# A fused attention, router and feed-forward kernel: set-up moved to GpSimd, identity transposes added, and the order of the expert stage's side work changed

## The chip, the cores and the metric

The kernel runs on one core of one Trainium2 chip. The metric is the device time of one execution in microseconds; before the change three executions took 980.26, 981.56 and 983.67 us (median 981.56). One more execution was profiled: it took 980.59 us, of which 978.8 us lie between its first and its last instruction (the span). Engine names: PE is TensorE's matrix products and PEld its weight loads, DVE is VectorE, ACT is ScalarE, POOL is GpSimd, SP is the engine that issues most transfers.

## What is computed

Three parts run one after the other, all in float32:

```python
# attention: 4 batches, 8 heads, 576 positions, 64 columns a head
scores = q @ k.T / sqrt(64)
keep   = scores >= scores.max(-1) - tau          # others count as minus infinity
x      = softmax(scores where kept) @ v          # reshaped to 2304 tokens x 512
# one of 8 experts for each token
logits = x @ w_gate + modality_bias[modality_id]
e      = argmax(logits);  g = softmax(logits)[e]
x      = g * (relu(x @ w1[e]) @ w2[e])           # 512 -> 1024 -> 512
# a dense layer for all tokens
h = x @ w_in                                     # 512 -> 2048
out = (h * sigmoid(1.702 * h)) @ w_out           # 2048 -> 512
```

Most products are made of several products of rounded parts (a high and a low part of each operand), so that the float32 accuracy is kept.

## The kernel before

**Attention** goes over 16 pairs of heads, four a batch, with nine units of work a pair. `Attention.run` (from L404) handles two units in each pass of its loop, so there are 72 passes and one closing pass; pass numbers below count from 0. In a pass, TensorE makes the scores of two units (`qk`, L234) into one of two PSUM buffers, and transposes the masked scores of the two units of the pass before (`trans`, L302). VectorE takes the row maximum (`max`, L245), ScalarE the exponential (`exp`, L251), VectorE the mask and row sum (`mask`, L275), which frees the PSUM buffer for the next scores but one. After that come a few matrix products with V from a list (`avq`), work on the rows of a finished half batch (`rowq`), and one entry of `poolq`, then the list `side`.

`poolq` holds the preparation of the operands of later pairs (`split`, L137): for each half of a pair's columns GpSimd scales the query rows (L143), rounds keys and queries into `kA` (L144) and forms the rest `kB` (L145). After the second half, `place` issues four transfers on SP (L154 to L157) that bring the parts to the partitions where they are multiplied; L156 writes over what L154 reads, and L157 over what L155 reads. In pass 0 four entries are put there, two for pair 1 and two for pair 2; one entry runs in each pass. Pair 1 is first used by the second unit of pass 4.

Each engine takes its instructions in the order in which the program issues them, and there is no planner: the order is written out by hand, with constants for how many entries of each list a pass takes.

`side` is a list of small pieces of work that `sides(n)` (L492) takes from the front, up to n at a call; a `None` ends the call, and is taken off. During attention a pass takes one. At the start the list holds seven `None`, then `gate_setup`, the clearing of a block of rows that is then written to memory ten times (`extra`), and the router's seven set-up pieces (`setup_items`, L543: `loads`, `ids`, `parts`, `tables`, `order`, `modality`, `bias`), which prepare counters, comparison tables and the bias of each token. These fall into passes 19 to 25. Later entries are the router's own work on a batch (`gate_items`) and, after the third and the fourth batch, the assignment of tokens to slots of 512 rows of one expert (`assign`, phases A and B).

**Assignment B** ranks the tokens of each expert, finds a place for each, and turns places into lists of token numbers. It compares a counter with each token's place to build `OL` (`low`, L845, three instructions), builds `R` (`high`, L851), multiplies `R` by two tables of token number digits (`values(0)` and `values(1)`, L858, both on GpSimd in phase B), and multiplies `OL` with `R` on TensorE (`sum_up`), from which `lists` makes the indices called `gB`.

**The expert stage** has five slots s of eight steps f each (the loop from L1308). In a step (`Ffn.step`) TensorE multiplies the tokens with 128 columns of w1 (`s1`, 12 products, L945), ScalarE and VectorE form the rounded activation and its rest (L1149, L1150), and TensorE makes the second product of the step two before (`s2`, 12 products, L967), in which the second product of the first group already needs the low part of w2 (`bl`). The weights of the next steps are split into high and low parts by ScalarE and VectorE (`split` in `slot`, L1185, L1186). In steps 3 to 6 the next slot's tokens are transposed (`xprep`, L929, into the one PSUM buffer `av`), copied by ScalarE (L931) and completed by VectorE (L932); the next transpose waits for the buffer. Meanwhile the dense layer's weights, 64-bit numbers, are read and converted (`convert`, L1078 to L1105) in 15 pieces that go through `Pipe` `conv`: load, `upper` (three VectorE operations, L1090 to L1092), `lower` (four, L1101 to L1105). `conv` starts a piece in each odd step and does its halves as it goes. Each step also calls `sides` twice, with 9 after the first product's activation and with 12 at its end, and so works off assignment B from slot 0 on. Slot 2 is the first that needs `gB`: at slot 1, step 1, the program takes from `side` until `gB` is there.

**The dense layer** goes over the tokens in five blocks of 16 steps, with the same `Ffn`, and converts what is left of the weights in its first block.

Of the kernel before, what the change touches and what calls it, by code (L numbers as in the profile page):

```python
# [8 lines left out]
F32 = mybir.dt.float32  # L9
# [4 lines left out]
ACTF = mybir.ActivationFunctionType  # L14
ALU = mybir.AluOpType
# [6 lines left out]
NE = 8  # L22
# [3 lines left out]
PJ = 9  # L26
# [6 lines left out]
NS0 = 7  # L33
# [3 lines left out]
HO = True  # L37
# [2 lines left out]
NBW = 6  # L40
F0 = (0, 1, 0)
NROW = 2
SN = 1
SD = (1, 2, 2, 2, 1)
TAU_MAX = 104.0
# [2 lines left out]
class Attention:  # L48
# [88 lines left out]
    def split(self, p, i, pieces):  # L137

        nc = self.nc
        d = self.st[p]  # L140
        n = 640 // pieces
        A, B_, F = (self.heads(d[x], n, i * n) for x in ("kA", "kB", "F"))
        nc.gpsimd.tensor_scalar_mul(F[64:128], F[64:128], self.cq[64:128, 0:1])  # L143
        nc.gpsimd.tensor_copy(A, F)  # L144
        nc.gpsimd.tensor_sub(B_, F, A.bitcast(F32))  # L145
        if i == pieces - 1:
            self.place(p)
# [256 lines left out]
    def run(self):  # L404
        nc = self.nc
        NU = NPAIR * UPP
        self.load_first()
        self.load(1)
        rest = self.first()
        self.load_v(0)  # L410
        self.load_v(1)
        self.load(2)
        self.poolq = []
        self.avq, self.rowq, self.side = avq, rowq, side = [], [], []
        side += [None] * NS0 + [self.gate_setup, *self.extra] + self.router.setup_items(self.setup)
        it = done = 0
        while done < NU:
            last = it >= IT_LAST
            us = [u for u in (2 * it, 2 * it + 1) if u < NU]
            ts = [u for u in (2 * it - 2, 2 * it - 1) if 0 <= u < NU]  # L420
            starts = [u // UPP for u in us if u % UPP == 0]
            for p in starts:
                if p + 3 < NPAIR:
                    self.load(p + 3)
                if p + 2 < NPAIR:
                    self.load_v(p + 2)
                for n in range(1 if p == 0 else p + 2, min(p + 3, NPAIR)):
                    self.operands(n)
                    self.poolq += [lambda n=n, i=i: self.split(n, i, NPC) for i in range(NPC)]
            copies = []  # L430
            for i in range(2):
                if i < len(us):
                    self.qk(us[i])
                if i < len(ts):
                    copies += self.trans(ts[i])
                if i == 0 and not last:
                    n = AV1[it % 9]
                    while n and avq:
                        avq.pop(0)()
                        n -= 1  # L440
            for i in range(2):
                for c in range(2):
                    if CO[c] == 2 * i and c < len(copies):
                        copies[c]()
                if i < len(us):
                    self.max(us[i])
                    self.exp(us[i])
                for c in range(2):
                    if CO[c] == 2 * i + 1 and c < len(copies):
                        copies[c]()  # L450
                if last:
                    self.sides(SD[i], False)
            while rest:
                rest.pop(0)()
            for i, u in enumerate(us):
                self.mask(u)
                if last:
                    self.sides(SD[i + 2], False)
            n = AVL[it - IT_LAST] if last else AV[it % 9]
            while n and avq:  # L460
                avq.pop(0)()
                n -= 1
            for u in ts:
                self.trans_tails(u)
            n = ROWL[it - IT_LAST] if last else ROW[it % 9]
            while n and rowq:
                rowq.pop(0)()
                n -= 1
            n = 1
            while n and self.poolq:  # L470
                self.poolq.pop(0)()
                n -= 1
            self.sides(SD[4] if last else SN)
            for u in ts:
                done = u + 1
                p, w = divmod(u, UPP)
                if w == UPP - 1:
                    avq += self.av_items(p)
                    if p % 2:
                        avq.append(lambda b=p // HP, hh=p % HP // 2: rowq.extend(self.row_items(b, hh)))  # L480
            it += 1
# [33 lines left out]
PG = 512  # L515
# [7 lines left out]
class Router:  # L523
# [19 lines left out]
    def setup_items(self, tmp_pool):  # L543
# [56 lines left out]
            nc.vector.tensor_scalar(i2[:, 1], iaf, 63, None, op0=ALU.bitwise_and)  # L600

        def tables():
            nc.vector.tensor_copy(self.idp, i2)
            nc.vector.tensor_scalar(self.tri, self.iota, pf[:, 0:1], None, op0=ALU.is_gt)
            nc.vector.tensor_scalar(self.rev, self.iota[:, 0:NE], -1.0, float(NE), op0=ALU.mult, op1=ALU.add)

        def order():
            e = self.iota[:, 0:NE]
            nc.vector.tensor_tensor(
                self.before, e.unsqueeze(2).broadcast_to([128, NE, NE]), e.unsqueeze(1).broadcast_to([128, NE, NE]),  # L610
                op=ALU.is_gt)
            nc.vector.tensor_scalar_mul(self.pages, e, float(PG))

        def modality():
            nc.vector.tensor_copy(midf[0:64], mi[:, :, 0:PJ:2, 0])
            nc.vector.tensor_copy(midf[64:128, :, 0:4], mi[:, :, 1:PJ:2, 0])
            nc.vector.tensor_scalar(nmid, flat, -1.0, 1.0, op0=ALU.mult, op1=ALU.add)

        def bias():
            nc.vector.tensor_mul(self.bias, wide(flat.unsqueeze(2)), wide(bb[:, 1:2, :]))  # L620
            nc.vector.tensor_mul(tmp, wide(nmid.unsqueeze(2)), wide(bb[:, 0:1, :]))
            nc.vector.tensor_add(self.bias, self.bias, tmp)

        return [loads, ids, parts, tables, order, modality, bias]

    def gate_items(self, b, lgt):
        nc, wk = self.nc, self.c
# [64 lines left out]
    def assign(self, ph, gate):  # L692
# [161 lines left out]
            )  # L854

        def values(i):
            eng = nc.vector if i and first else nc.gpsimd
            eng.tensor_mul(R[:, :, i, :], R[:, :, 1, :], self.idp[:, i, 0:n].unsqueeze(2).broadcast_to([128, n, nh]))  # L858

        def sum_up(c0, c1):  # L860
# [129 lines left out]
def moe_kernel(ctx, tc, kq, v, tau, mid, w_gate, mod_bias, w1, w2, w_in, w_out, out):  # L990
    nc = tc.nc
# [316 lines left out]
    for s in range(NS):  # L1308
        blk = blocks[s]
        for f in range(8):  # L1310
            ffn.step(blk, f, (lambda: blk["split"](0, 1)) if f == 1 and HO else None, mid3=lambda: att.sides(9))
            f0 = F0[min(s, 2)]
            if s + 1 < NS and f in (f0, f0 + 1):
                if f == f0:
# [25 lines left out]
            if conv is None:  # L1340
                if not att.tail(6):
                    open_resident()
                    wi, wo = R["wi"], R["wo"]
                    conv = Pipe(
                        [piece("i", i, wi, i) for i in range(NWI)] + [piece("o", i, wo, i) for i in range(NWO)])
            elif f % 2 == 1 or len(conv.live) > 1:
                conv.step(f % 2)
            for _ in range((XP0 if s == 0 else XP)[f]):
                if xq:
                    xq.pop(0)()  # L1350
            att.sides(12)
    conv.drain()
    convert_loads(2)

# [127 lines left out]
```

## Time and profile before

| what | value |
|---|---|
| device time, three executions | 980.26, 981.56, 983.67 us |
| profiled execution | 980.59 us, span 978.8 us |
| PE busy | 930.2 us (95%) |
| PEld busy | 750.0 us (77%) |
| DVE busy | 556.3 us (57%) |
| ACT busy | 448.8 us (46%) |
| POOL busy | 237.7 us (24%) |
| mean granted clock of TensorE | 0.985 |

Busy time is the sum of an engine's instructions, as the profiler saw them; a busy PE is one with a product in its pipeline, not one at its peak. The granted clock is the share of full speed that the chip's throttle let TensorE have: 1.00 is 2.4 GHz, 0.50 is 1.2 GHz. In the rows below, a line such as L234 is a line of the kernel, `out<-in` names its tiles, x3 counts merged instructions, and a bracket gives the idle time of the engine just before and who ended it.

### The profile page before, as it was taken

How to read it: one execution, taken by the hardware profiler on the slowest of the kernel's cores; microseconds unless marked ns; L12 is line 12 of the kernel's file. 1: busy time of each engine (PE TensorE's matmuls, PEld its weight loads, DVE VectorE, ACT ScalarE, POOL GpSimd, SP SyncE). 2: the span in 40 equal slices, each digit the busy share in tenths (PEclk: the TensorE clock that was granted, in tenths of full speed). 3: DMA queues.
4: the chain of work that ended last, by engine and by line, in shares of the span. 5: the costliest groups of instructions: out<-in, count | busy, mean ns of one | idle time of the engine just before them, and what ended most of it. 6: DMA issues, size and time to landing. Idle time of an engine off the chain costs nothing. (4 is left out here: it accounts for less than half of the span.)

```text
span 978.8 us, 13986 instructions
## 1 busy us (share of the span) xinstructions
PE 930.2 (95%) x5009; PEld 750.0 (77%) x5009; DVE 556.3 (57%) x1194; ACT 448.8 (46%) x803; POOL 237.7 (24%) x322
## 2 busy tenths in 40 slices
PE   7899899999988969999999999999999999999994
PEld 6677777777765758878888888888888888888884
DVE  5888888888795497787766479961111111111110
ACT  4677677777775424444444434542222222222221
POOL 5935465576404422020302010010001000100100
PEclk7999999999999989999999999999999999999998
DMA  6766654655505434556555135330011000100100
GB/s 198 168 193 171 150 145 116 162 145 132 120 2 157 135 90 171 172 197 211 175 162 180 57 96 163 108 108 1 1 44 44 1 1 22 44 1 1 44 1 24
DMA packets 61307, 100.59 MB, mean 103 GB/s; under 512 B 9073, under 2 KB 32625, under 8 KB 61234
## 3 DMA queue, kind: packets, MB, share of 16 engines
q1 hardware_dynamic: 57394, 87.15, 31.1%
q0 software_dynamic: 3840, 12.50, 3.8%
q8 instruction: 42, 0.69, 0.3%
q14 instruction: 31, 0.25, 0.1%
HBM read 63.99 MB, written 17.23 MB: 83 GB/s over the span
## 5 line engine op out<-in xcount | busy, mean ns | idle before, releaser
L1161 DVE TENSOR_TENSOR hl<-sg,hh 128x512 fp32r<-128x512 f32 (+1 forms) x80 | 51.0, 638 | 242.9 <-ACT hh L1159 242.9
L1158 ACT ACTIVATE sg<-tr 128x512 f32<-128x512 f32 (+1 forms) x80 | 44.3, 554 | 208.4 <-PE tr L945 207.0
L245 DVE TENSOR_SCALAR_CACHE_REDUCE e<-sc,taue 128x576 f32<-128x576 f32 x144 | 116.3, 813 | 31.1 <-PE sc L234 27.3
L251 ACT ACTIVATE e<-e,thr 128x576 f32<-128x576 f32 x144 | 111.1, 776 | 31.3 <-DVE e L245 30.6
L234 PE MATMUL sc<-kA,qT 128*128 128x288 f32 x320 | 104.4, 342 | 20.7 <-DVE E L275 16.3
L945 PE MATMUL tr<-xh,wi_h 128*128 128x512 f32 (+1 forms) x320 | 120.6, 377 | 0.0
L945 PE MATMUL tr<-xh,wi_l 128*128 128x512 f32 (+1 forms) x320 | 118.8, 371 | 0.0
L945 PE MATMUL tr<-xl,wi_h 128*128 128x512 f32 (+1 forms) x320 | 118.7, 371 | 0.0
L967 PE MATMUL sc<-wo_h,hl 128*128 128x512 f32 x288 | 113.8, 395 | 0.0
L967 PE MATMUL sc<-wo_l,hh 128*128 128x512 f32 x288 | 113.7, 395 | 0.0
L967 PE MATMUL sc<-wo_h,hh 128*128 128x512 f32 x288 | 113.5, 394 | 0.0
L275 DVE SCALAR_TENSOR_TENSOR E<-sc,thr,e 128x576 f32<-128x576 f32 x128 | 103.4, 815 | 8.4 <-ACT e L251 5.0
L304 ACT COPY AT<-tr 128x512 f32<-128x512 f32 x128 | 73.9, 577 | 43.3 <-PE tr L302 43.2
L234 PE MATMUL sc<-kB,qT 128*128 128x288 f32 x320 | 91.2, 301 | 0.5 <-DVE kB L215 0.5
L234 PEld LDWEIGHTS sc<-kA,qT 128*128 128x128 f32 x320 | 61.7, 193 | 37.7 <-issue 21.9
L302 PE MATMUL tr<-ident,E 128*128 128x128 f32 x512 | 79.2, 278 | 0.0
L348 PE MATMUL av<-AT,V 128*64 128x288 f32 x512 | 76.7, 419 | 0.0
L945 PEld LDWEIGHTS tr<-xh,wi_l 128*128 128x128 f32 x320 | 60.2, 188 | 11.4
L945 PEld LDWEIGHTS tr<-xl,wi_h 128*128 128x128 f32 x320 | 60.3, 188 | 11.2
L945 PEld LDWEIGHTS tr<-xh,wi_h 128*128 128x128 f32 x320 | 60.2, 188 | 11.1
L302 PEld LDWEIGHTS tr<-ident,E 128*128 128x128 f32 x512 | 64.3, 144 | 0.6 <-DVE r L284 0.4
L967 PEld LDWEIGHTS sc<-wo_h,hl 128*128 128x128 f32 x288 | 54.0, 187 | 13.0
(215 smaller groups left out, 1754.2 us busy)
## 6 DMA issues: line engine op xcount, KB each, us to landing
ra<-in_moe_w_dram SPq DMA_DIRECT2D x20, 512.0 KB, 5.6
rb<-in_moe_w_dram SPq DMA_DIRECT2D x20, 512.0 KB, 3.8
F<-in_kq_dram SPq DMA_DIRECT2D x15, 640.0 KB, 5.3
cv_raw<-in_moe_w_in_dram SPq DMA_DIRECT2D x16, 512.0 KB, 5.0
cv_raw<-in_moe_w_out_dram SPq DMA_DIRECT2D x16, 512.0 KB, 3.6
V<-in_vp_dram SPq DMA_DIRECT2D x16, 320.0 KB, 4.9
kA<-kA SPq DMA_DIRECT2D x15, 320.0 KB, 3.4
kB<-kB SPq DMA_DIRECT2D x15, 320.0 KB, 3.5
```

What stands on the lines that cost most here:

```text
L234: nc.tensor.matmul(sc[:, hf, 0:288], l, d[kk][:, c0 + hf * 288:c0 + (hf + 1) * 288], start=(i == 0), stop=(i == len(ops) - 1),)
L245: nc.vector.tensor_scalar(e, d["sc", w][:, :, 0:288], self.taue[:, 0:1], 3.0e38, op0=ALU.add, op1=ALU.min, accum_out=thr)
L251: self.nc.scalar.activation(d["e", w], d["e", w], ACTF.Exp, bias=d["thr", w][:, 0:1], scale=-1.0)
L275: nc.vector.scalar_tensor_tensor(out=E.rearrange("p (a c) -> p a c", a=2), in0=d["sc", w][:, :, 0:288], scalar=d["thr", w][:, 0:1], in1=d[ ...
L302: nc.tensor.transpose(tp[:, kc * 128:(kc + 1) * 128], E[:, k0 + kc * 128:k0 + (kc + 1) * 128], self.ident)
L304: copies.append(lambda: nc.scalar.copy(AT[:, h, :, c * 128:(c + 1) * 128], tp.rearrange("p (k c) -> p k c", k=4)))
L348: nc.tensor.matmul(d["av"][h * 64:(h + 1) * 64, 0:288], d["V"][:, h, kc, :], d["AT"][:, h, kc, hf * 288:(hf + 1) * 288], start=False, stop ...
L945: nc.tensor.matmul(hps[:, 0:T], w[:, kd, :], blk[x][:, kd, :], start=(i == 0), stop=(i == 11))
L967: nc.tensor.matmul(y, h[:, cs], w, start=(f == 0 and i == 0), stop=(f == blk["nf"] - 1 and i == 2))
L1158: nc.scalar.activation(sg, hps, ACTF.Gelu_apprx_sigmoid)
L1161: return [upper, lambda: nc.vector.tensor_sub(hl, sg, hh.bitcast(F32))]
```

## The change

Seven edits are made together.

1. A list `FILL` gives numbers for passes 0 to 4 of attention; so many transposes of the identity matrix are issued in each of these passes after the masks, into the PSUM buffer `av`. Nobody reads their result.
2. For pair 1 alone, the scaling in `split` is issued on ScalarE in place of GpSimd. In pass 0 two entries of `poolq` run in place of one.
3. The router's set-up pieces come before the cleared rows in `side`, so they fall into passes 8 to 15, with one `None` added after `ids`; the cleared rows fall into passes 16 to 26.
4. `tables`, `modality` and `bias`, and one operation of `order`, are issued on GpSimd in place of VectorE. `parts` and the comparison of `order` stay on VectorE.
5. In `assign`, phase B, both products of `values` are issued on VectorE in place of GpSimd; phase A is as before.
6. `conv` takes no step until `gB` is there.
7. In the expert stage `sides` is called with 6 and 6 in place of 9 and 12.

```diff
+FILL = (14, 12, 12, 12, 4)
...
-        nc.gpsimd.tensor_scalar_mul(F[64:128], F[64:128], self.cq[64:128, 0:1])
+        if p == 1:
+            nc.scalar.activation(F[64:128], F[64:128], ACTF.Copy, scale=self.cq[64:128, 0:1])
+        else:
+            nc.gpsimd.tensor_scalar_mul(F[64:128], F[64:128], self.cq[64:128, 0:1])
...
-        side += [None] * NS0 + [self.gate_setup, *self.extra] + self.router.setup_items(self.setup)
+        side += [None] * NS0 + [self.gate_setup, *self.router.setup_items(self.setup), *self.extra]
...
+            if it < len(FILL) and FILL[it]:
+                warm = self.ps_av.tile([128, 512], F32, name="av")
+                for _ in range(FILL[it]):
+                    nc.tensor.transpose(warm[:, 0:128], self.ident, self.ident)
...
-            n = 1
+            n = 1 if it else 2
             while n and self.poolq:
...
         def tables():
-            nc.vector.tensor_copy(self.idp, i2)
-            nc.vector.tensor_scalar(self.tri, self.iota, pf[:, 0:1], None, op0=ALU.is_gt)
-            nc.vector.tensor_scalar(self.rev, self.iota[:, 0:NE], -1.0, float(NE), op0=ALU.mult, op1=ALU.add)
+            nc.gpsimd.tensor_copy(self.idp, i2)
+            nc.gpsimd.tensor_scalar(self.tri, self.iota, pf[:, 0:1], None, op0=ALU.is_gt)
+            nc.gpsimd.tensor_scalar(self.rev, self.iota[:, 0:NE], -1.0, float(NE), op0=ALU.mult, op1=ALU.add)
...
-            nc.vector.tensor_scalar_mul(self.pages, e, float(PG))
+            nc.gpsimd.tensor_scalar_mul(self.pages, e, float(PG))
...
         def modality():
-            nc.vector.tensor_copy(midf[0:64], mi[:, :, 0:PJ:2, 0])
+            nc.gpsimd.tensor_copy(midf[0:64], mi[:, :, 0:PJ:2, 0])
...
         def bias():
-            nc.vector.tensor_mul(self.bias, wide(flat.unsqueeze(2)), wide(bb[:, 1:2, :]))
+            nc.gpsimd.tensor_mul(self.bias, wide(flat.unsqueeze(2)), wide(bb[:, 1:2, :]))
...
-        return [loads, ids, parts, tables, order, modality, bias]
+        return [loads, ids, None, parts, tables, order, modality, bias]
...
         def values(i):
-            eng = nc.vector if i and first else nc.gpsimd
+            eng = nc.gpsimd if first and not i else nc.vector
...
-            ffn.step(blk, f, (lambda: blk["split"](0, 1)) if f == 1 and HO else None, mid3=lambda: att.sides(9))
+            ffn.step(blk, f, (lambda: blk["split"](0, 1)) if f == 1 and HO else None, mid3=lambda: att.sides(6))
...
-            elif f % 2 == 1 or len(conv.live) > 1:
+            elif "gB" in router.idx and (f % 2 == 1 or len(conv.live) > 1):
                 conv.step(f % 2)
...
-            att.sides(12)
+            att.sides(6)
```

## Rows read from the trace of the kernel before

**Rows 1.** Busy time of each engine in stretches, with the granted clock (PEclk).

```profile
core 0: us, PE busy (x) PEld busy (x) DVE busy (x) ACT busy (x) POOL busy (x), PEclk, DMA share, GB/s
11.80:21.80 10.00, 8.00 (x34) 7.54 (x34) 6.62 (x18) 3.77 (x6) 8.86 (x7) 0.50 0.65 229
107.00:110.00 3.00, 3.00 (x13) 2.70 (x13) 1.33 (x6) 2.13 (x6) 1.92 (x3) 0.52 0.38 143
363.36:366.70 3.34, 3.34 (x11) 2.81 (x12) 3.31 (x5) 0.59 (x1) 0.00 (x0) 0.53 0.18 20
405.00:410.00 5.00, 5.00 (x25) 4.08 (x24) 4.86 (x9) 2.23 (x5) 0.00 (x0) 1.00 0.31 98
```

**Rows 2.** Timeline of TensorE, first passes (start, us, engine, line, tiles, [idle before <-releaser]).

```profile
4.44 3.06 PEld L194 LDWEIGHTS tr<-ident 128*128 128x128 f32 x15
8.28 0.29 PE L234 MATMUL sc<-kA,qT 128*128 128x288 f32 x1
12.90 0.58 PE L234 MATMUL sc<-kA,qT 128*128 128x288 f32 x1 [2.93 <-DVE E L275]
17.76 0.58 PE L234 MATMUL sc<-kA,qT 128*128 128x288 f32 x1 [0.90 <-DVE E L275]
22.62 0.37 PE L234 MATMUL sc<-kA,qT 128*128 128x288 f32 x1 [0.59 <-DVE E L275]
23.10 0.49 PEld L302 LDWEIGHTS tr<-ident,E 128*128 128x128 f32 x4
26.13 0.37 PE L234 MATMUL sc<-kA,qT 128*128 128x288 f32 x1 [1.32 <-DVE E L275]
```

**Rows 3.** Timeline of GpSimd, ScalarE and SP: the operands of pairs 0 and 1.

```profile
12.44 1.90 POOL L143 TENSOR_SCALAR F<-F,cq 64x640 f32<-64x640 f32 x1 [10.50 <-DMA F<-in_kq_dram]
16.86 1.89 POOL L143 TENSOR_SCALAR F<-F,cq 64x640 f32<-64x640 f32 x1
6.36 0.73 ACT L214 CAST kA<-F 128x640 fp32r<-128x640 f32 x1 [1.03 <-DMA F<-in_kq_dram]
24.37 0.59 SPq L157 DMA_DIRECT2D kB<-kB  x1
```

**Rows 4.** Timeline around the router's set-up, and the same pass of each nine.

```profile
68.90 0.40 PE L234 MATMUL sc<-kA,qT 128*128 128x288 f32 x1 [0.43 <-DVE E L275]
102.25 1.56 DVE L603 CAST idp<-i 128x40 bf16<-128x40 int32 x1
102.21 1.56 POOL L145 TENSOR_TENSOR kB<-F,kA 128x640 fp32r<-128x640 f32 x1
106.60 0.40 PE L234 MATMUL sc<-kA,qT 128*128 128x288 f32 x1 [1.87 <-DVE E L275]
143.79 0.40 PE L234 MATMUL sc<-kA,qT 128*128 128x288 f32 x1 [0.41 <-DVE E L275]
179.37 0.40 PE L234 MATMUL sc<-kA,qT 128*128 128x288 f32 x1 [0.43 <-DVE E L275]
```

**Rows 5.** Timeline of the expert stage's slot 0, with two step marks of slot 1.

```profile
363.36 0.90 PE L929 MATMUL av<-ident,xg 128*128 128x128 f32 x3 [7.43 <-DVE xl L932]
341.36 0.20 DVE L725 TENSOR_TENSOR cmpp<-cnt,pages 128x40 f32<-128x40 f32 x1
350.40 0.82 DVE L845 TENSOR_TENSOR OL<-iota,plf 128x640 bf16<-128x640 f32 x1
350.40 6.16 DVE L845 TENSOR_TENSOR OL<-iota,plf 128x640 bf16<-128x640 f32 x3
350.56 4.65 POOL L858 TENSOR_TENSOR R<-R,idp 128x960 bf16<-128x960 bf16 x2 [13.26 <-DVE R L851]
357.57 1.22 DVE L1186 TENSOR_TENSOR al<-ra,ah 128x1024 fp32r<-128x1024 f32 x1
362.62 0.68 DVE L932 SCALAR_TENSOR_TENSOR xl<-av,xh 128x512 fp32r<-128x512 f32 x1
392.02 0.60 ACT L1149 ACTIVATE hh<-tr 128x512 fp32r<-128x512 f32 x1 [1.66 <-PE tr L945]
397.62 0.60 ACT L1149 ACTIVATE hh<-tr 128x512 fp32r<-128x512 f32 x1 [0.39 <-PE tr L945]
```

More of the change, by code (lines that the diff above doesn't have):

```diff
@@ L611, in order @@
                 op=ALU.is_gt)
-            nc.vector.tensor_scalar_mul(self.pages, e, float(PG))
+            nc.gpsimd.tensor_scalar_mul(self.pages, e, float(PG))
         def modality():
-            nc.vector.tensor_copy(midf[0:64], mi[:, :, 0:PJ:2, 0])
-            nc.vector.tensor_copy(midf[64:128, :, 0:4], mi[:, :, 1:PJ:2, 0])
-            nc.vector.tensor_scalar(nmid, flat, -1.0, 1.0, op0=ALU.mult, op1=ALU.add)
+            nc.gpsimd.tensor_copy(midf[0:64], mi[:, :, 0:PJ:2, 0])
+            nc.gpsimd.tensor_copy(midf[64:128, :, 0:4], mi[:, :, 1:PJ:2, 0])
+            nc.gpsimd.tensor_scalar(nmid, flat, -1.0, 1.0, op0=ALU.mult, op1=ALU.add)
         def bias():
-            nc.vector.tensor_mul(self.bias, wide(flat.unsqueeze(2)), wide(bb[:, 1:2, :]))
-            nc.vector.tensor_mul(tmp, wide(nmid.unsqueeze(2)), wide(bb[:, 0:1, :]))
-            nc.vector.tensor_add(self.bias, self.bias, tmp)
-        return [loads, ids, parts, tables, order, modality, bias]
+            nc.gpsimd.tensor_mul(self.bias, wide(flat.unsqueeze(2)), wide(bb[:, 1:2, :]))
+            nc.gpsimd.tensor_mul(tmp, wide(nmid.unsqueeze(2)), wide(bb[:, 0:1, :]))
+            nc.gpsimd.tensor_add(self.bias, self.bias, tmp)
+        return [loads, ids, None, parts, tables, order, modality, bias]
     def gate_items(self, b, lgt):
```

## Prediction

> **What bounds the kernel now.** I read the busy time by stretches first, because its granted clock shows where TensorE ran at 1.2 GHz, then TensorE's timeline, whose brackets say who ended each idle time, and last the other engines' timelines around the long idle times. TensorE is the bound nearly everywhere. In the expert stage a stretch can have 5.00 us of TensorE in 5.00 while VectorE, at 4.86, holds nothing up [rows 1], and in mid-attention nine passes (two pairs) take 179.37 − 143.79 = 35.58 us with waits of some 0.4 us a piece [rows 4]. So what is worth anything is time in which TensorE stands still or runs at half clock. There are three such places, and the seven edits fall on them.
>
> (a) The first passes. TensorE waits 2.93 us before pass 1 and the clock is 0.50 from 11.8 to 21.8 us. Passes 1 and 2 take 4.86 us each (12.90 to 17.76 to 22.62); pass 3, back at full clock, takes 3.51 with 1.32 idle in it [rows 1, 2].
> (b) The router's set-up. A cast of 40 columns takes VectorE 1.56 us: it starts 0.04 us after GpSimd's L145 and ends with it. The mask that the next pass needs is late, TensorE idles 1.87 us and then runs from 107 to 110 at 0.52 [rows 1, 4].
> (c) Slot 0 of the expert stage. TensorE stands 7.43 us until VectorE has written `xl`, then works 3.34 us at a clock of 0.53 [rows 1, 5]. VectorE is at work all the while: `OL` takes 6.16 us, of which the first instruction, issued before GpSimd's products of `R`, takes 0.82; the others run beside those products (4.65 us) and stretch. Then come a weight split (1.22) and, up to `xl` at 362.62, seven operations of the conversion [rows 5].
>
> **The change, part by part.**
>
> *Edit 1, identity transposes.* One costs 0.49/4 = 0.122 us at full clock (four of L302) and 3.06/15 = 0.204 at half (fifteen of L194) [rows 2]. The 14 in pass 0 are 1.7 us at full clock, inside the 2.93 of idle; pass 1 begins at 12.90 as before. If the clock stays up, passes 1 to 3 each need what pass 3 needs without its idle time, 3.51 − 1.32 = 2.19, and 12 × 0.122 = 1.47 on top: 3.66, 0.15 more than the chain over VectorE and ScalarE asks. Together 3 × 3.66 = 11.0 against 4.86 + 4.86 + 3.51 = 13.2: a gain of 2.25. The 4 of pass 4 are 0.5 us, and a wait like pass 3's hides them; bare, they cost that. Their PSUM buffer is free until pass 5 and nobody reads it. Bounds: no held clock and 12 × 0.204 = 2.4 us a pass (a rival, below), or the clock held and all of it hidden, 2.7.
>
> The clock rose the first time by 8.28 us (a product of 0.29 there, 0.58 at 12.90), after fifteen transposes had filled 4.44 to 7.50, with hardly a product between [rows 2]. So here transposes do seem to count as work. The Trainium skill (TensorE: Matmul & The Clock Gate, Part 4: PE-mode transpose) says otherwise: transposes do not count as engine activity in the same way, and full clock does not engage for them. By that rule edit 1 would cost time; by the rows it gains 2.25. The rows stand nearer to this case.
>
> *Edit 2, ScalarE's scaling for pair 1.* GpSimd needs 4.42 us for one half (12.44 to 16.86), 1.90 of it scaling; ScalarE's cost is bounded by its cast of twice the partitions, 0.73, and by GpSimd's 1.90. I take 0.73, the nearest. Both halves are then done at 12.44 + 0.73 + 2 × 2.52 = 18.2 instead of 21.3: 3.1 us earlier, and so are the transfers chained behind them (the last issued at 24.37) [rows 3]. Pass 4, which needs them, comes 2.25 earlier. So the edit gains nothing by itself; without it, edit 1 would run into a wait. ScalarE's queue is held until the pair's data are there (12.44), and the next instruction behind is a copy of transposes from pass 1, after 14 us. GpSimd, relieved of 3.8 us, does pair 2 earlier; nobody waits for that.
>
> *Edits 3 and 4, set-up.* Nine passes took 106.60 − 68.90 = 37.70, and the next nine 143.79 − 106.60 = 37.19, against 35.58 undisturbed: 2.12 and 1.61, together 3.73 us, the second being the slow clock [rows 1, 4]. Ten operations leave VectorE and four stay (three of `parts`, one of `order`). On GpSimd the ten have no row here: between 0.2 and 1.90 us each, 2 to 19 us; near the low end, since the 1.90 is for 640 columns and the largest of these has 160. Behind them in GpSimd's queue are operands of pair 5, not used before pass 22; even 19 us fit. The four that stay can each be held up as the cast was: 0 to 1.56 each. `ids` has a pass more before `parts`, and passes 11 and 12 hold no split, so I take 0.3 in all. Gain 3.4, bounds 1.5 and 3.7. The two small loads and ten row writes that change places on SP have its 0.59 of issue time each [rows 3] and stand in front of loads three pairs ahead: nothing, with that cover; the `None` puts the set-up's end at pass 15, ten passes earlier than now.
>
> *Edits 5 to 7, slot 0.* I counted off the list. Before, with 9 and 12, step 3 ends with `high`, all of `OL`, both products and the gate in one go; steps 3 to 5 also hold two conversions. With 6 and 6, ranking falls to step 3's middle, `high`, the first `OL` and first product to the end of step 4, the rest to the middle of step 5, `sum_up` and `lists` to the middle of slot 1's step 0: one step before `gB` is asked for, so the forced taking never runs. A step takes TensorE 5.60 (392.02 to 397.62 [rows 5]), with its token transposes (four at 0.49 [rows 2]) about 6.1.
>
> VectorE without GpSimd beside it: `OL` 0.82 + 0.82 + 1.5 (twice the columns) = 3.2 instead of 6.16. A product of `R` (960 columns) on VectorE: 0.82 for 640 gives about 1.2; upper bound 2.3, GpSimd's own. I take 1.2. Weight split 1.22, `xl` and `hl` 0.7 each, small operations 0.2 each [rows 5]. Step 3: 0.7 + 1.0 + 1.2 + 0.7 + 1.0 = 4.6. Step 4: 0.7 + 1.7 + 1.2 + 0.7, then `places`, `digits` 0.5, `high` 1.2, `OL` 0.8, product 1.2 = 8.0. Step 5: 0.7, then 0.8 + 1.2 + 1.5 + 0.5, split 1.2, `xl` 0.7 = 6.6. Step 6: 2.6. In sum 21.8 in 4 × 6.1 = 24.4 us of TensorE, but steps 4 and 5 bunch: 14.6 in 12.2. `hl` has two steps to spare; the low half of w2 has not. With step 3 at 0, `hl` of step 5 starts at about 17.3 instead of 15.7, the middle portion ends at 22 and `bl` at 23; TensorE asks for it in step 6 at 18.3 + 2.8 + 0.2 = 21.3. That leaves a stall of about 1.5 us, too short to expect a slow clock by (b). Bounds: 0 (VectorE catches up) and 3.8 with a clock fall (each product 2.3).
>
> Gone are 7.43 and what the slow clock cost, 3.34 × (1 − 0.53) = 1.6; new is 1.5. Gain 7.5, bounds 4 and 9.
>
> The three conversions not done in slot 0 (seven operations, about 3.9 us each: 357.57 + 1.22 to 362.62) come in slot 4, in the rhythm of slots 1 to 3, the last half after it. Their cover is VectorE's slack: 4.86 of 5.00 busy beside conversions left TensorE at 5.00 [rows 1]. I count nothing; bare, they cost 11.8.
>
> **Sum.** 2.25 + 3.4 + 7.5 = 13.2. The profiled execution took 980.59 (span 978.8, 1.8 around it): 967.4. The median of the three runs is 1.0 higher, which gives 968.4; I name 967.5.
>
> **Rivals.**
> - *The transposes don't hold the clock.* For it: passes 1 and 2, in part transposes, ran slow. Against: the first rise. Price: the 2.25 is not gained, and passes 1 and 2 grow by 2 × 2.4 minus their idle 0.90 and 0.59 = 3.4. Total 967.4 + 5.7 = 973.1. Chance 0.10. (It is the rule of the Trainium skill's page named under edit 1.)
> - *The slot 0 stall is shortened, not removed*: products of `R` at 2.3 each, `bl` 2.2 later, a stall of 3.7 and a clock fall of 1.6: 967.4 + 3.8 = 971.2. For it: steps 4 and 5 bunch. Against: VectorE's 0.82 for 640 columns. Chance 0.17.
> - *The set-up still catches VectorE*: `parts` and `order` are not moved, and one blocked operation was all it took. Gain 0 instead of 3.4: 970.8. Against: the passes without a split. Chance 0.07.
> - *The held conversions are bare* (slower). VectorE is the bound in slot 4, the 11.8 us stand on the path, and two clock falls of 1.6 follow: 967.4 + 15.0 = 982.4. It decides from 13.2 us bare. Against: slots 1 to 3 did the same beside weight splits, and slot 4 has fewer. Chance 0.03.
>
> My forecast has 0.63: its own range, from the bounds, 964.5 to 970.5. The range for 8 in 10 reaches to the first three rivals: 963.5 to 973.5. A change within 0.3% (2.9 us) is what a measurement here can't tell from none; that needs two of the three gains to fail together: 0.03. Slower 0.04, faster 0.93.
>
> **What would show it.** Right: granted clock 1.00 from 11.8 to 21.8 and pass 4 near 23.9; no cast of 1.56 on VectorE and nine-pass times near 35.6 throughout; `OL` at 0.8, 0.8 and 1.5; no idle time over 2 us in slot 0; TensorE full in slot 4. Wrong: a clock of 0.50 after 12 us with transposes in it; a wait for `bl` or `xl` over 4 us; idle time in slot 4 or in the dense layer's first block.

## The result, and the profile after

The changed kernel took 967.94 us in the median of four runs (966.63 to 969.42) against 981.61 for the kernel before: a ratio of 0.9857, 95% interval 0.9839 to 0.9876. Forecast were 967.5 and a range of 963.5 to 973.5. The profiled execution took 968.38 with a span of 966.6; the sum on the profiled basis was 967.4.

Lines have moved: the product of queries and keys is L238 (was L234), the mask L279, the added transposes of the identity L466 (those at L198, L194 before, stand in both kernels), the weight split L1194, the second product of the experts L975, `xl` L940. The first view is the busy time by stretches of the kernel after; the last columns are the granted clock, the DMA share and GB/s.

```profile
11.80:21.80 10.00, 8.59 (x71) 8.41 (x72) 9.16 (x24) 7.39 (x13) 8.08 (x7) 1.00 0.87 272
102.00:105.00 3.00, 3.00 (x22) 2.56 (x24) 2.37 (x7) 2.57 (x7) 1.38 (x3) 1.00 1.03 302
354.00:357.50 3.50, 3.50 (x12) 2.70 (x11) 0.22 (x1) 0.00 (x0) 0.00 (x0) 0.52 0.57 137
```

Against [rows 1]: the two slow stretches of attention are gone. A slow stretch in slot 0 is still there, at another place and behind another wait. TensorE's timeline of the first passes, against [rows 2]:

```profile
4.45 2.58 PE L198 MATMUL tr<-ident 128*128 128x128 f32 x15
7.00 0.40 PE L238 MATMUL sc<-kA,qT 128*128 128x288 f32 x1
...
9.96 1.69 PE L466 MATMUL av<-ident 128*128 128x128 f32 x14
13.05 0.37 PE L238 MATMUL sc<-kA,qT 128*128 128x288 f32 x1 [1.40 <-DVE E L279]
...
15.05 1.47 PE L466 MATMUL av<-ident 128*128 128x128 f32 x12
...
25.83 0.37 PE L238 MATMUL sc<-kB,qT 128*128 128x288 f32 x1 [0.26 <-DMA kB<-kB]
...
28.20 0.37 PE L238 MATMUL sc<-kA,qT 128*128 128x288 f32 x1 [0.88 <-DVE ET L279]
```

Fourteen transposes take 1.69 and the pass begins within 0.15 us of when it did, as worked out; the wait before it shrinks from 2.93 to 1.40. Passes 1 to 3 take 3.63, 3.51 and 3.51 (13.05, 16.68, 20.19, 23.70). In pass 4 TensorE waits 0.26 for `kB`, an operand of pair 1. Pass 5 begins at 28.20 instead of 30.42: 2.22 us gained. The set-up in GpSimd's and TensorE's timelines, against [rows 4]:

```profile
56.14 0.22 POOL L611 CAST idp<-i 128x40 bf16<-128x40 int32 x1 [6.84 <-DVE i L608]
```

```profile
101.90 0.40 PE L238 MATMUL sc<-kA,qT 128*128 128x288 f32 x1 [0.42 <-DVE E L279]
...
137.46 0.40 PE L238 MATMUL sc<-kA,qT 128*128 128x288 f32 x1 [0.42 <-DVE E L279]
...
173.03 0.40 PE L238 MATMUL sc<-kA,qT 128*128 128x288 f32 x1 [0.41 <-DVE E L279]
```

The cast that held VectorE for 1.56 us takes GpSimd 0.22. The nine passes from 66.36 take 35.54, the next two nines 35.56 and 35.57; the nine up to 66.36, which now hold `parts` and `tables`, take 34.65, where the kernel before took 34.96 (33.94 to 68.90). At 137.46 the kernel is 6.33 us ahead of [rows 4]'s 143.79, 2.22 of that from the start. Slot 0, VectorE and then TensorE, against [rows 5]:

```profile
345.68 0.82 DVE L853 TENSOR_TENSOR OL<-iota,plf 128x640 bf16<-128x640 f32 x1
346.41 1.15 DVE L866 TENSOR_TENSOR R<-R,idp 128x960 bf16<-128x960 bf16 x1
...
348.08 0.82 DVE L853 TENSOR_TENSOR OL<-iota,plf 128x640 bf16<-128x640 f32 x1
349.88 1.49 DVE L853 TENSOR_TENSOR OL<-iota,plf 128x1280 bf16<-128x1280 f32 x1
...
351.82 1.20 DVE L1194 TENSOR_TENSOR bl<-rb,bh 128x1024 fp32r<-128x1024 f32 x1
```

```profile
353.07 0.50 PE L975 MATMUL sc<-bl,hh 128*128 128x512 f32 x1 [1.93 <-DVE bl L1194]
...
354.50 0.63 PE L975 MATMUL sc<-bh,hh 128*128 128x512 f32 x1
```

The wait of 7.43 us for `xl` has become one of 1.93 for `bl`. Behind it the products go on at full clock for a microsecond (the second to fourth take 0.40) and then take 0.63. The slot's marks in ScalarE's timeline, two before the change and two after it:

```profile
325.13 0.60 ACT L1149 ACTIVATE hh<-tr 128x512 fp32r<-128x512 f32 x1 [2.34 <-PE tr L945]
386.45 0.60 ACT L1149 ACTIVATE hh<-tr 128x512 fp32r<-128x512 f32 x1 [0.77 <-PE tr L945]
```

```profile
318.50 0.60 ACT L1157 ACTIVATE hh<-tr 128x512 fp32r<-128x512 f32 x1 [2.34 <-PE tr L953]
372.83 0.60 ACT L1157 ACTIVATE hh<-tr 128x512 fp32r<-128x512 f32 x1 [4.01 <-PE tr L953]
```

Slot 0's first activation came at 325.13 before and 318.50 now; slot 1's second at 386.45 and 372.83: the slot gained 13.62 − 6.63 = 7.0. Last, slot 4, on VectorE and TensorE:

```profile
529.95 0.69 DVE L1100 SCALAR_TENSOR_TENSOR cv_a<-cv_raw,cv_a 128x512 int32<-128x512 int32 x1
530.55 0.68 DVE L940 SCALAR_TENSOR_TENSOR xl<-av,xh 128x512 fp32r<-128x512 f32 x1
```

```profile
531.29 0.66 PE L937 MATMUL av<-ident,xg 128*128 128x128 f32 x4 [0.62 <-DVE xl L940]
```

A held conversion stands ahead of `xl`, and TensorE waits 0.62. Between its activations of steps 4 and 7 slot 4 gives back 0.9 (the lead over the kernel before falls from 13.47 to 12.54); 12.2 are left at the end.

### The profile page after: what moved, and what is told of

Read it like the earlier page. It is cut to its first block, busy times and chain, and to the rows that moved or that the text cites. A ratio compares the mean times of both kernels' runs of the same rounds, so it can differ in the third digit from the quotient of the medians.

```text
span 966.6 us, 14095 instructions
## 1 busy us (share of the span) xinstructions
PE 929.9 (96%) x5063; PEld 749.5 (78%) x5063; DVE 550.8 (57%) x1186; ACT 449.9 (47%) x805; POOL 229.4 (24%) x328
## 5 line engine op out<-in xcount | busy, mean ns | idle before, releaser
L238 PE MATMUL sc<-kA,qT 128*128 128x288 f32 x320 | 102.1, 336 | 14.0 <-DVE E L279 10.7
L975 PE MATMUL sc<-wo_h,hl 128*128 128x512 f32 x288 | 113.8, 395 | 0.0
L975 PE MATMUL sc<-wo_l,hh 128*128 128x512 f32 x288 | 113.7, 395 | 0.0
L975 PE MATMUL sc<-wo_h,hh 128*128 128x512 f32 x288 | 113.5, 394 | 0.0
L279 DVE SCALAR_TENSOR_TENSOR E<-sc,thr,e 128x576 f32<-128x576 f32 x128 | 103.6, 815 | 8.4 <-ACT e L255 4.5
L238 PE MATMUL sc<-kB,qT 128*128 128x288 f32 x320 | 89.3, 295 | 1.2 <-DVE kB L219 0.9
L238 PEld LDWEIGHTS sc<-kA,qT 128*128 128x128 f32 x320 | 60.2, 188 | 30.8 <-issue 20.8
L306 PE MATMUL tr<-ident,E 128*128 128x128 f32 x512 | 76.7, 272 | 0.0
L953 PEld LDWEIGHTS tr<-xh,wi_h 128*128 128x128 f32 x320 | 60.2, 188 | 11.2
L975 PEld LDWEIGHTS sc<-wo_h,hl 128*128 128x128 f32 x288 | 54.0, 187 | 13.0
L975 PEld LDWEIGHTS sc<-wo_h,hh 128*128 128x128 f32 x288 | 54.1, 188 | 12.2
```

Of the source, the lines that this page charges most:

```text
L238: nc.tensor.matmul(sc[:, hf, 0:288], l, d[kk][:, c0 + hf * 288:c0 + (hf + 1) * 288], start=(i == 0), stop=(i == len(ops) - 1),)
L279: nc.vector.scalar_tensor_tensor(out=E.rearrange("p (a c) -> p a c", a=2), in0=d["sc", w][:, :, 0:288], scalar=d["thr", w][:, 0:1], in1=d[ ...
L306: nc.tensor.transpose(tp[:, kc * 128:(kc + 1) * 128], E[:, k0 + kc * 128:k0 + (kc + 1) * 128], self.ident)
L953: nc.tensor.matmul(hps[:, 0:T], w[:, kd, :], blk[x][:, kd, :], start=(i == 0), stop=(i == 11))
L975: nc.tensor.matmul(y, h[:, cs], w, start=(f == 0 and i == 0), stop=(f == blk["nf"] - 1 and i == 2))
```

## The experiments

Each run is the changed kernel but for its edit. What the clock did once can weigh 2 us in a total, so the runs are compared by stages: "slot 0" is the time from its first activation to slot 1's second, 61.32 before (386.45 − 325.13) and 54.33 after (372.83 − 318.50).

**No transposes.**

```diff
-FILL = (14, 12, 12, 12, 4)
+FILL = (0, 0, 0, 0, 0)
```

> The changed kernel without any identity transpose in passes 0 to 4. Theory (the transposes hold the clock): TensorE stands about 2.9 us before pass 1, the clock is 0.50 for some 10 us from about 12 us on, passes 1 and 2 take 4.4 to 4.9 us each instead of 3.6, pass 4 starts at 25.5 to 26.2 instead of 23.7, and the later stages follow 1.8 to 2.4 us behind. Rival (transposes do not count as work and something else, such as GpSimd's earlier operands, kept the clock up): pass 4 starts at 23.2 to 23.8 and the clock stays at 1.00.

Measured: 967.03, span 965.3. TensorE's timeline, and a stretch:

```profile
13.01 0.37 PE L238 MATMUL sc<-kA,qT 128*128 128x288 f32 x1 [2.93 <-DVE E L279]
...
17.42 0.37 PE L238 MATMUL sc<-kA,qT 128*128 128x288 f32 x1 [0.89 <-DVE E L279]
```

```profile
13.80:17.20 3.40, 2.72 (x13) 2.30 (x11) 2.32 (x6) 2.19 (x4) 3.23 (x4) 0.54 0.99 370
```

The clock does fall behind the wait of 2.93, but for 3.4 us and not 10: one slow pass of 4.41 and then passes of 3.51. Pass 5 starts at 28.48, so all 54 transposes together are worth 0.28 us against this execution, or 0.8 by passes 1 to 3 alone, as this one has no wait for `kB` in pass 4. Slot 0's wait for `bl` was 1.62 here, and no clock fell behind it: that, not the transposes, is why the total is below the change's.

**Transposes in pass 0 only.**

```diff
-FILL = (14, 12, 12, 12, 4)
+FILL = (14, 0, 0, 0, 0)
```

> Only the 14 transposes of pass 0 are left; passes 1 to 4 have none. Theory A (one long gap is what lets the clock fall; gaps of 1.3 us a pass do not): clock 1.00 throughout, passes 1 to 3 take 3.51 each as pass 3 did before the change, pass 4 starts at 23.4 instead of 23.7. Theory B (a wait of 1.93 us was enough in slot 0, so gaps of 1.3 us a pass are enough as well): the clock falls between 15 and 20 us and pass 4 starts at 24.5 to 26.

Measured: 965.01, span 963.2. TensorE's timeline, and the stretch of [rows 1]:

```profile
9.78 1.69 PE L466 MATMUL av<-ident 128*128 128x128 f32 x14
12.88 0.37 PE L238 MATMUL sc<-kA,qT 128*128 128x288 f32 x1 [1.41 <-DVE E L279]
...
16.50 0.37 PE L238 MATMUL sc<-kA,qT 128*128 128x288 f32 x1 [1.47 <-DVE E L279]
...
27.55 0.37 PE L238 MATMUL sc<-kA,qT 128*128 128x288 f32 x1 [1.33 <-DVE ET L279]
```

```profile
11.80:21.80 10.00, 6.34 (x48) 5.95 (x49) 9.03 (x24) 7.65 (x14) 8.13 (x7) 1.00 0.91 281
```

The fourteen of pass 0 alone keep the clock at 1.00, though TensorE now idles 1.1 to 1.5 us before each pass. Pass 5 starts 0.93 earlier than with none and 0.65 earlier than with all; at 136.86 against 137.46 the lead is still 0.6. That lead is not the price of the other 40 transposes: 0.17 of it was there at pass 1, passes 1 to 3 take 3.62, 3.52 and 3.50, as they do with all 54, and the rest arises in pass 4, where this execution does not wait for `kB`. With all 54 and pair 1 scaled on ScalarE the wait there is up to 0.57 in the runs below, and 0.85 in one of the two others that have only the fourteen. So the 40 neither gained nor cost anything that these runs can tell.

**Pair 1 scaled on GpSimd again.**

```diff
-        if p == 1:
+        if p < 0:
```

> Pair 1's scaling back on GpSimd, all else as changed. Theory (edit 2 is what lets edit 1 count): GpSimd ends pair 1's halves at about 21.3 instead of 18, the transfers land about 3 us later, and the second unit of pass 4, which waited 0.26 us for them, waits 2.5 to 3.3 us; pass 5 starts at 30.3 to 31 instead of 28.2 and the end comes 1.8 to 2.5 us later. Rival (GpSimd has slack there): no wait over 0.5 us, pass 5 at 28.2.

Measured: 970.34, span 968.6. TensorE's timeline:

```profile
26.74 0.37 PE L238 MATMUL sc<-kA,qT 128*128 128x288 f32 x1 [1.56 <-DMA kA<-kA]
...
28.92 0.37 PE L238 MATMUL sc<-kB,qT 128*128 128x288 f32 x1 [1.81 <-DMA kB<-kB]
...
31.30 0.58 PE L238 MATMUL sc<-kA,qT 128*128 128x288 f32 x1 [0.47 <-DVE ET L279]
```

Pass 4 waits 1.56 and 1.81 us for operands, and then the clock falls (0.58 for a product instead of 0.37). Slot 0 begins at 322.56 instead of 318.50: edit 2's scaling is worth 4.06, more than the whole start gained, and more than the 1.8 to 2.5 expected, since the clock fell too. Its second entry of `poolq` in pass 0 was not undone.

**Portions of 9 and 12 again.**

```diff
-            ffn.step(blk, f, (lambda: blk["split"](0, 1)) if f == 1 and HO else None, mid3=lambda: att.sides(6))
+            ffn.step(blk, f, (lambda: blk["split"](0, 1)) if f == 1 and HO else None, mid3=lambda: att.sides(9))
...
-            att.sides(6)
+            att.sides(12)
```

> The router's portions back at 9 and 12 in the expert stage, with the conversions still held and the products of R on VectorE. Theory (the hold and the products do the work; the smaller portions put the tables ahead of the low half of w2 in step 5 and so make the wait of 1.93 us): all of the tables fall at the end of step 3, where the first activation's rest has two steps to spare; no wait for the low half, no clock fall, the indices are there in step 6 of slot 0, one conversion more is done in slot 0, and the time is 2.5 to 4.5 us below the changed kernel's (span 962 to 964). Rival (smaller portions are needed): TensorE waits 2 to 6 us for VectorE in slot 0, span 967 to 971.

Measured: 970.89, span 969.1. TensorE's timeline, slots 0 and 3:

```profile
341.13 0.50 PE L975 MATMUL sc<-bl,hh 128*128 128x512 f32 x1 [0.69 <-DVE bl L1194]
...
350.86 0.66 PE L937 MATMUL av<-ident,xg 128*128 128x128 f32 x4 [0.89 <-DVE xl L940]
...
507.85 0.44 PE L953 MATMUL tr<-xl,ah 128*128 128x384 f32 x1 [1.13 <-DVE xl L940]
```

Slot 0 shows waits of 0.19, 0.86 (for the ranks' prefix on GpSimd), 0.69 and 0.89 instead of one, no slow clock, and takes 54.19. With 6 and 6 it takes 52.42 where the clock stays (the change once more, below): the smaller portions are worth 1.8 there. My theory that they were not needed fell. A second effect I had not seen: with large portions the lists are there one step sooner, so the first conversion is loaded in step 7 of slot 0 instead of slot 1, and all of them stand in other steps. From slot 1's second activation on, there are four waits for `xl` of 0.57 to 1.13 and the rest takes 596.67 instead of 593.83.

**Set-up early as in the change, all on VectorE** (the ten operations of edit 4 back).

```diff
-            nc.gpsimd.tensor_copy(self.idp, i2)
+            nc.vector.tensor_copy(self.idp, i2)
...
-            nc.gpsimd.tensor_add(self.bias, self.bias, tmp)
+            nc.vector.tensor_add(self.bias, self.bias, tmp)
```

> The set-up stays early (passes 8 to 15), but its ten operations are issued on VectorE again. Theory (what hurt was one VectorE operation held up by a GpSimd instruction, so the pass counts and the engine hardly does): GpSimd is idle in passes 11 and 12, the cast takes about 0.2 us, no wait of TensorE over 0.7 us, and the nine passes that hold the set-up take at most 0.5 us more than in the changed kernel. Rival (VectorE has no room for set-up in any pass): 2 to 4 us more, with a wait of over 1 us and possibly a slow clock.

Measured: 968.86, span 967.1. VectorE's timeline, GpSimd's and TensorE's:

```profile
72.07 0.31 DVE L629 TENSOR_TENSOR tmpb<-nmid,bb 128x160 f32<-128x160 f32 x1
72.41 1.55 DVE L630 TENSOR_TENSOR bias<-bias,tmpb 128x160 f32<-128x160 f32 x1
```

```profile
72.05 1.73 POOL L149 TENSOR_TENSOR kB<-F,kA 128x640 fp32r<-128x640 f32 x1
```

```profile
76.48 0.40 PE L238 MATMUL sc<-kA,qT 128*128 128x288 f32 x1 [1.58 <-DVE E L279]
```

The theory fell: the cast takes 0.18 in its new place, but an addition of 160 columns is caught in its stead: 1.55 beside GpSimd's subtraction, where a like operation 0.3 us earlier took 0.31. TensorE waits 1.58 for the next masks. Slot 0 begins 2.2 later, 0.26 of that from the start: edit 4 is worth about 2.

**Set-up late as before, on GpSimd** (edit 3 back; the `None` goes too).

```diff
-        side += [None] * NS0 + [self.gate_setup, *self.router.setup_items(self.setup), *self.extra]
+        side += [None] * NS0 + [self.gate_setup, *self.extra] + self.router.setup_items(self.setup)
...
-        return [loads, ids, None, parts, tables, order, modality, bias]
+        return [loads, ids, parts, tables, order, modality, bias]
```

> The set-up is late again (after the cleared rows, passes 19 to 25), but its ten operations are on GpSimd. Theory (the held-up cast on VectorE was the loss): nine-pass times stay within 0.6 us of 35.6, as the three operations of parts, which wait about 1 us for GpSimd's counters, are all that is left. Rival (it is the late place, where VectorE must wait for GpSimd's counters and for its splits): TensorE waits more than 1 us near pass 21 or 22 and nine passes take 36.5 to 39.

Measured: 967.58, span 965.8. VectorE's and TensorE's timelines:

```profile
96.16 0.24 DVE L605 COPY ia<-ib 64x20 int32<-64x20 int32 x1 [1.02 <-POOL ib L598]
```

```profile
99.29 0.37 PE L238 MATMUL sc<-kA,qT 128*128 128x288 f32 x1 [0.67 <-DVE ET L279]
```

Here `parts` comes a pass too soon and VectorE stands 1.02 us for GpSimd's `ids`; TensorE waits 0.67. Slot 0 begins 0.84 later, though the start was 0.2 earlier. Edit 3 with its `None` is worth about 1.

**The table products on GpSimd again.**

```diff
-            eng = nc.gpsimd if first and not i else nc.vector
+            eng = nc.vector if i and first else nc.gpsimd
```

> Both products of R in phase B back on GpSimd. Theory (VectorE's OL is held up while a GpSimd product runs): the second and third OL take 1.5 to 3 us each instead of 0.82 and 1.49, the low half of w2 comes 1 to 2 us later, the wait for it in step 6 of slot 0 is 2.5 to 4 us instead of 1.6 to 1.9, and the clock falls after it. Rival (VectorE gains more from not making the products, 2 x 1.15 us, than it loses): the wait is under 1 us.

Measured: 966.81, span 965.0. VectorE's timeline, and GpSimd's:

```profile
346.82 4.81 DVE L853 TENSOR_TENSOR OL<-iota,plf 128x640 bf16<-128x640 f32 x2
...
352.09 1.20 DVE L1194 TENSOR_TENSOR bl<-rb,bh 128x1024 fp32r<-128x1024 f32 x1
```

```profile
345.65 4.64 POOL L866 TENSOR_TENSOR R<-R,idp 128x960 bf16<-128x960 bf16 x2 [13.31 <-DVE R L859]
```

Beside GpSimd's products the two `OL` operations, 640 and 1280 columns, take 4.81 instead of 0.82 + 1.49 = 2.31. That costs 2.5; VectorE saves two products at 1.15. Counted from the slot's first activation `bl` starts 0.46 later, TensorE waits 2.08, and no clock fell: less than the theory and more than the rival had. From slot 0's first activation to slot 1's first 46.66 us pass, against 45.87 to 46.22 in six other runs with this slot's code and no fall: edit 5 is worth 0.4 to 0.8.

**Conversions not held.**

```diff
-            elif "gB" in router.idx and (f % 2 == 1 or len(conv.live) > 1):
+            elif f % 2 == 1 or len(conv.live) > 1:
```

> The conversions run from slot 0, step 1, as before the change; portions 6 and 6. Theory (two conversions of 4 us fall into the steps with the tables, and VectorE has no room): TensorE waits 5 to 9 us in slot 0 with a slow clock, and slot 4 is rid of its 0.62 us wait; in sum 4 to 8 us more than the changed kernel. Rival (the small portions alone take the stall away): under 2.5 us of waits in slot 0, and in sum 0 to 1 us less.

Measured: 972.17, span 970.4. TensorE's timeline, and a stretch:

```profile
348.89 0.66 PE L937 MATMUL av<-ident,xg 128*128 128x128 f32 x4 [1.13 <-DVE xl L940]
...
357.93 0.80 PE L975 MATMUL sc<-bl,hh 128*128 128x512 f32 x1 [5.35 <-DVE bl L1194]
```

```profile
355.00:360.00 5.00, 2.07 (x5) 1.68 (x6) 4.86 (x9) 0.00 (x0) 2.81 (x5) 0.51 0.04 4
```

Conversions stand on VectorE ahead of the tables, so `bl` is 5.35 us late and the clock falls. Slot 0 takes 59.38: 5.05 more than after, both with a fall of the clock. Slot 4 has no wait for `xl`, and the rest from slot 1 on is 1.3 shorter: held conversions have a price, and edit 6 is worth 3.7 net. Against the change's second execution (below), whose clock did not fall, it is 5.6.

**The change once more, and the kernel before once more**, unaltered.

> The changed kernel once more, unaltered. Theory A (the clock's fall behind the 1.9 us wait for the split operand in slot 0 is chance: it came in one of seven executions whose wait was 1.6 to 2.1 us): profiled span 963.5 to 967, the stretch from slot 0's first activation to slot 1's 45.9 to 46.2 us where the clock stays and 47.8 where it falls; time 965 to 969. Theory B (this kernel's own instruction order brings the fall): the fall is there again behind a wait of 1.9, the stretch is 47.8 and the span 966.6.

> The kernel before once more, to see how long its clock is low behind the 2.93 us wait at the end of pass 0: 10 us (11.8 to 21.8) in the execution shown, against 3.4 us in the changed kernel without its transposes, behind a wait of the same 2.93. Theory A (the length of the fall is chance, so the transposes' worth differs from execution to execution): pass 1 to pass 5 takes between 15.6 and 17.5 us, and the span is 976.5 to 979. Theory B (it belongs to the kernel before, whose passes wait for other reasons): 10 us again, pass 5 at 30.4, span 978.8.

Measured: the change 966.76 in the median of four (966.38 to 968.74), ratio 0.9854 (0.9834 to 0.9873), span 964.6; the kernel before 982.95, span 981.1. TensorE's timeline and a stretch of the change's second execution, then a stretch of before's:

```profile
352.60 0.50 PE L975 MATMUL sc<-bl,hh 128*128 128x512 f32 x1 [1.63 <-DVE bl L1194]
```

```profile
354.00:357.50 3.50, 3.50 (x19) 2.87 (x18) 0.00 (x0) 0.00 (x0) 0.00 (x0) 1.00 0.69 163
```

```profile
11.80:21.80 10.00, 7.90 (x33) 7.50 (x34) 6.62 (x19) 3.83 (x7) 8.49 (x7) 0.50 0.64 220
```

The change's own instruction order does not bring the fall each time: with a wait of 1.63 slot 0 ran at full clock and took 52.42, 1.9 less. Whether another wait of 1.93 would bring it was not seen. For the kernel before, the 10 slow us at the start were the same again, as in theory B. But this is hardly a second draw: in both executions the fifteen transposes from 4.4 us on took 3.46 us and the clock rose between 8.0 and 8.3, while in the run without transposes they took 2.94 and the first product behind them, at 7.14, was fast. So chance is not excluded. The run with transposes in pass 0 only also began with 3.46, and its clock held. Slot 0 of the kernel before came out otherwise this time, 63.64 us long, with two waits (1.92 for `bl`, 5.81 for `xl`) and a clock fall with each.

**Transposes in pass 0 only, portions of 1 and 11**; then the same with the operand's preparation ahead of the conversion.

```diff
-FILL = (14, 12, 12, 12, 4)
+FILL = (14, 0, 0, 0, 0)
...
-            ffn.step(blk, f, (lambda: blk["split"](0, 1)) if f == 1 and HO else None, mid3=lambda: att.sides(6))
+            ffn.step(blk, f, (lambda: blk["split"](0, 1)) if f == 1 and HO else None, mid3=lambda: att.sides(1))
...
-            att.sides(6)
+            att.sides(11)
```

```diff
+            for _ in range((XP0 if s == 0 else XP)[f]):
+                if xq:
+                    xq.pop(0)()
             if conv is None:
...
-            for _ in range((XP0 if s == 0 else XP)[f]):
-                if xq:
-                    xq.pop(0)()
```

> The changed kernel with transposes in pass 0 only (14, 0, 0, 0, 0) and portions of 1 entry in the middle of a step and 11 at its end, so that the step whose split operand was waited for has two table products and one entry's work ahead of the split rather than six entries'. Theory A (the wait of 1.6 to 1.9 us goes, and no fall of the clock can follow it): slot 0's first activation at 317.8, from there to slot 1's first 44.0 to 44.6 us, span 961 to 962.5, time 963 to 964.5. Theory B (the same work only moves to the next step's end and is waited for there, as with portions of 9 and 12): 45.9 or more, span 963.2 or more.

> The kernel with 1 and 11 entries, and in each step the next slot's operand preparation is issued ahead of the held conversion instead of behind it. Theory A (slot 4's wait of 0.62 us and its 0.9 us are VectorE's conversion standing ahead of the low part of the operand): slot 4 gives back nothing, span 0.6 to 1 below the kernel with 1 and 11 alone. Theory B (the conversion then stands ahead of the next step's split operand instead): a wait for the split operand of 0.3 to 1 us appears in slots 1 to 4, span the same or up to 1 above.

Measured: 965.54 (965.30 to 965.73, ratio 0.9834, 0.9818 to 0.9851) and 964.07 (963.90 to 964.46, ratio 0.9821, 0.9804 to 0.9837), four runs each beside the change's 966.76. VectorE's timeline and TensorE's of the second:

```profile
529.20 0.69 DVE L940 SCALAR_TENSOR_TENSOR xl<-av,xh 128x512 fp32r<-128x512 f32 x1
529.80 0.42 DVE L1109 TENSOR_SCALAR cv_e<-cv_a 128x512 int32<-128x512 int32 x1
```

```profile
351.71 0.50 PE L975 MATMUL sc<-bl,hh 128*128 128x512 f32 x1 [1.16 <-DVE bl L1194]
```

The first expectation held in part, with 45.44 us to slot 1's first activation, between its two theories: the wait for `bl` shrank from 1.61 to 1.16 and did not go, since `high`, two `OL` and two products now run in one go ahead of the split. Slot 0 took 51.97, 0.45 less than 52.42; the start was 1.2 later than with pass 0's transposes alone, behind a DMA (0.85 for `kB`). The second held: `xl` before the conversion, no wait in slot 4, no new one for `bl`; from slot 0's first activation it is 0.7 quicker than its neighbour up to slot 4's fifth, and 1.3 up to slot 4's last. In the totals this shows less: between the dense layer's 18th and 57th activations the neighbour and the run with transposes in pass 0 only took 220.5 us, and all other executions 221.3, though no edit touches that stretch; why is open. It is the fastest version, 17.6 us below the kernel before, and its runs lie clear of the change's.

## Why the prediction was right, and where it was off

By marks, the lead over the kernel before: 2.2 at pass 5, 6.3 at 137 us, 6.6 at slot 0's start, 13.6 at slot 1's second activation, 13.5 in slot 4's step 4, 12.5 at its end, 12.2 at the end. The sum said 2.25, then 5.65, then 13.15 to the end. It came out near for partly compensating reasons, and partly by luck: between the two profiled executions of each kernel (spans 978.8 and 981.1 before, 966.6 and 964.6 after) the gain is anything from 12.2 to 16.5, and nearly all of that spread arises in slot 0 (61.32 and 63.64 before, 54.33 and 52.42 after).

- *Start, 2.25 forecast, 2.22 measured, wrongly credited.* The step that edit 2 "gains nothing by itself" fails. That edit 1 would run into a wait without it was right, but given no price: two waits and a clock fall, 4.06. The order of the transfers was right, their moment less so: the first was issued 3.2 earlier (16.36 against 19.56), the last 2.26 (22.11 against 24.37), and `kB` still came 0.26 late. And in the run without any transposes 1.94 of the 2.22 are still there, because the clock was then low for 3.4 us and not 10. "So here transposes do seem to count as work" holds: fourteen in pass 0 kept the clock at 1.00 where without them it fell to 0.50. By the rule of the Trainium skill (TensorE: Matmul & The Clock Gate, Part 4: PE-mode transpose) full clock does not engage for transposes; for these the measurement decides against it, and the rival of 973.1 is out. In the timeline after, full clock also engaged among transposes: the first product, at 7.00, took 0.40 (0.58 at the low clock), and TensorE had done nothing before it but transposes of the identity and two products of one column. The 12 a pass were costed at 0.15 over the chain; without them TensorE had 1.1 to 1.5 us of idle a pass, and passes 1 to 3 took as long with them as without. So passes 1 to 3 gained 2.6 in place of 2.25, and 0.4 were lost before pass 1 and in pass 4. Why the clock is low for 10 us in the kernel before and 3.4 without transposes, both behind 2.93 us of idle, stays open: a kernel without edits 1 and 2 both was not run, and the two began differently, as said above.
- *Set-up, 3.4 forecast, 4.1 measured.* The 0.3 set aside for the four operations left on VectorE was not needed (0.17 to 0.18 each in `parts`), and nine passes stand at 35.55, at the 35.58 of the undisturbed ones. Of the 4.1 some 0.3 came in the nine passes before, outside the sum. Edits 3 and 4 both count: moved early but left on VectorE, another operation was caught; late on GpSimd, VectorE stood for `ids`. That the set-up could still catch VectorE was a fair rival; with both edits it did not.
- *Slot 0, 7.5 forecast, 7.0 in the profiled execution.* The order of VectorE's work was right to the operation: `OL` 0.82, 0.82 and 1.49 against 0.8, 0.8 and 1.5, a product 1.15 against 1.2, and the new wait at `bl` in step 6, 1.93 against 1.5. The step that failed is "too short to expect a slow clock by (b)": (b)'s own wait was 1.87, and the stall came out at 1.93, 0.4 longer than its term, with a clock fall to 0.52 behind it. In six other runs with this slot's code the stall was 1.61 to 1.95 and no clock fell. Without the fall, in the second execution, the slot gained 8.9, and against the kernel before's second execution 11.2: that the term of 7.5 was met is in part luck. Of the second rival the clock fall happened, a product at 2.3 and a stall of 3.7 did not; even with products on GpSimd the wait was 2.08, as VectorE is spared as much as it loses.
- *Held conversions, 0 forecast, 1.4 lost* (13.6 to 12.2 in the marks, 0.9 of it in slot 4). "Their cover is VectorE's slack", read from slots 1 to 3, is too small in slot 4: it has three tiles, its steps are shorter (4.1 to 4.9 us between its first five activations, against 5.60), and a conversion ahead of `xl` costs a wait of 0.62. Issued behind `xl`, as in the last run, it costs none: from slot 1's second activation to the dense layer's 18th that run takes 265.72 us, against 267.29 after, 265.94 with conversions not held, and 265.83 before.

Worth of single edits, each undone alone in one execution: transposes 0.3 to 0.8, scaling 4.1, place of the set-up 1, its engine 2, products 0.4 to 0.8, holding 3.7 to 5.6, portions 4.6 (1.8 in slot 0, 2.8 behind it). These are 16 to 19 together, and the change gained 12.2 to 16.5 by span, 13.7 and 14.9 by the medians of the two comparisons. Each was undone with the others in place, so some may have taken from others what they gave; with a clock that fell in some executions and not in others, that is not shown.

## What to carry to other kernels

Where a dummy fills an idle stretch, find by leaving out which of its parts hold the clock; here one stretch of 1.7 us did all of it, and the rest changed nothing that showed. When work is put off into a later stage, compare the slack of each shape of that stage, not of the stage's mean, and ask what it stands ahead of on its engine. Before a small difference is put down to an edit, look whether it arises where the edit acts. Read a change of several edits by marks along the run: a total mixes the gains with whether the clock happened to fall behind one wait.

## What the runs showed of the hardware

A wait near 1.9 us sometimes brings a slow clock: it fell behind 1.87 (before, attention), 1.92 (before's second execution), 1.93 (after, to 0.52 for over 3 us), and 1.81 with another wait of 1.56 just ahead of it (scaling on GpSimd), and did not behind 1.95 (set-up on VectorE) and 2.08 (products on GpSimd), nor behind any of the waits of 1.61 to 1.72 for `bl`. After the end of such a wait TensorE could first go on at full speed, for a microsecond in after's timeline (353.07 to 354.1) and for half of one in the run without transposes, behind 2.93 us (13.01 to 13.6); in the kernel before the first product behind 2.93 us was already slow (0.58 at 12.90).

VectorE's stretching beside GpSimd's two-operand operations is not tied to one form: a cast of 40 columns (1.56 against 0.18), an f32 addition of 160 columns (1.55 against 0.31) and `OL` (4.81 for two against 2.31) all showed it.
